# The 64-row term of the output projection as pairs of half-height matmuls in every block, and one v matmul moved a step ahead

## The chip, the core and the metric

The kernel runs on one core of one Trainium2 chip. The metric is the device time of one execution in microseconds (us): 213.64 us is the median of three runs of the kernel before (213.34 to 214.03).

## What is computed

An input x of 2048 rows and 448 columns is normalised row by row, and two branches are added to it: attention with 16 heads of 28 over a sliding window of 256 keys, and a gated feed-forward layer with 1792 hidden columns.

```python
xn = _layernorm(x)
qkv = (xn @ wqkv).reshape(B, S, 3, H, Dh).transpose(2, 0, 3, 1, 4)   # H = 16, Dh = 28
scores = einsum("bhqd,bhkd->bhqk", q, k) * Dh ** -0.5
mask = (i - j >= 0) & (i - j < 256)
o = softmax(where(mask, scores, -1e9)) @ v
return x + o @ wo + (gelu(xn @ w_gate) * (xn @ w_up)) @ w_down
```

All tensors are bf16. 448 columns are three chunks of 128 rows and one of 64 for TensorE, whose array has 128 rows; that fourth chunk is what this change is about.

## The kernel before

The 2048 rows are four blocks (`NB`) of 512 columns (`QB`), each of four output tiles of 128. For each block `attention` runs nine or ten score steps and `gated` then makes the hidden values `hT`. One score step is: scores of four heads a time into the one score buffer (`sc`, half of PSUM), the exponential on ACT into `p_sb`, and masks on DVE (`apply_masks`; on GpSimd in block 0). A `plan`, written out by hand, says what TensorE does in each step while ACT works: `(d, 12)` is twelve steps of the generator `d`. `gen_down(qb - 1)` is the output of the block before, `gen_pairs` the q, k and v of the block after, and `gen_up` part of the up projection of the present one. Steps 4 and 6 begin with the product of probabilities and v (`pv`, tile `ov`); `"sums"` and `"inverse"` are DVE's row sums and reciprocals. The other half of PSUM is four banks, `take`n and `give`n back in turn; a tile that takes a bank waits for whatever still reads it.

In `gen_down` an output tile is the sum of 14 down terms (`hT` by `wd`) and four wo terms (`oN` by `wo`), each a matmul of 448 columns; `main` and `late` name the down terms and `os` the wo terms. `end` adds x on DVE and sends the tile out. The fourth wo term has 64 real rows. For tiles 0 and 1 of blocks 0 to 2 it is computed on two halves of the array at once: tile 0 on rows 0 to 63, tile 1 on rows 64 to 127, where `o_finish` puts a copy of tile 1's columns. Tiles 2 and 3 use a full matmul, with zeros in the lower rows. In the last block all four tiles do so; its tile 3 is cut into halves of 224 columns (`first`, `last`, tile `pl`), so that little is left at the very end.

`o_collect` and `o_deliver` take the values of heads 14 and 15 through DRAM into pad rows of `oN`; `o_finish` follows them. In `mm_half` and `chunk`, too, two matmuls of 64 rows run side by side. `v_dense(t, pv)` issues the three full chunks of the v product of tile t, `v_half` its fourth; in block 0 that of tile 2 is at the head of step 1's fill.

Of the kernel before, what the change touches and what calls it, by code (L numbers as in the profile page):

```python
# [17 lines left out]
P = 128  # L18
# [9 lines left out]
def kernel(  # L28
# [185 lines left out]
    def give(*tiles):  # L214
        for ps in tiles:
            spare.append(held.pop(id(ps))[0])


    def v_dense(t, pv):
        mm3(pv, lambda c: xnT[:, c, t * P:(t + 1) * P], lambda c: wv[:, c, :], True, False)  # L220

    def v_half(t, pv):
        mm_half(pv, xnT[:, 3, t * P:(t + 1) * P], wv[:, 3, :], t % 2, False, True)
# [133 lines left out]
    def o_finish(qb):  # L357

        oN = oNs[qb]
        if qb < NB - 1:  # L360
            nc.gpsimd.memset(oN[64:128, 3, 2 * P:QB], 0.0)
            nc.gpsimd.tensor_copy(out=oN[64:128, 3, P:2 * P], in_=oN[0:64, 3, P:2 * P])
        else:
            nc.gpsimd.memset(oN[64:128, 3, :], 0.0)

    def gen_down(qb):

        hT, oN = hTs[qb], oNs[qb]
        fs = [(hT, wd, f) for f in range(NF)]
        main, late, os = fs[0:5] + fs[7:12], [fs[f] for f in (5, 12, 6, 13)], [(oN, wo, g) for g in range(4)]  # L370

        def begin(tt, lo=0, up=D):
            return tt, take("po", up - lo), lo, up

        def end(tt, po, lo, up):
            t, w = 4 * qb + tt, up - lo
            if lo:
                res = work.tile([P, 2 * QB], bf16, name="res", tag="wa", bufs=1)
            else:
                res = work.tile([P, D], bf16, name="res", bufs=4)  # L380
            nc.vector.tensor_tensor(out=res[:, 0:w], in0=po[:, 0:w], in1=x_sb[:, t, lo:up], op=ALU.add)  # L381
            if id(po) in held:
                give(po)
            nc.sync.dma_start(out=outv[:, t, lo:up], in_=res[:, 0:w])
            last_res[:] = [res]

        def part(o, terms, start=False, stop=False):
            tt, po, lo, up = o
            w = up - lo
            for n, (x, wt, k) in enumerate(terms):  # L390
                nc.tensor.matmul(po[:, 0:w], lhsT=x[:, k, tt * P:(tt + 1) * P], rhs=wt[:, k, lo:up],  # L391
                                 start=start and n == 0, stop=stop and n == len(terms) - 1, skip_group_check=True)
                if stop and n == len(terms) - 1:
                    end(*o)
                yield

        def whole(terms, *o):
            yield from part(begin(*o), terms, True, True)

        if qb < NB - 1:  # L400
            two = [begin(tt) for tt in range(2)]
            for o in two:
                yield from part(o, main + late, True)
            for o in two:
                yield from part(o, os[0:3])
            for tt, po, *_ in two:
                r = slice(64 * tt, 64 * tt + 64)
                nc.tensor.matmul(po, lhsT=oN[r, 3, tt * P:(tt + 1) * P], rhs=wo[r, 3, :], start=False, stop=True,
                                 tile_position=(64 * tt, 0), skip_group_check=True)
            for o in two:  # L410
                end(*o)
            yield
            for tt in (2, 3):
                yield from whole(main + late + os, tt)
        else:
            two = [begin(tt) for tt in range(2)]
            for terms, start in ((main, True), (late, False)):
                for o in two:
                    yield from part(o, terms, start)
            first, last = ((3, phase[0].pool.tile([P, 2, QB], f32, name="pl", tag="s")[:, 0, 0:D // 2], lo, lo + D // 2)  # L420
                           for lo in (0, D // 2))
            yield from part(first, main + late, True)
            for o in (*two, first):
                yield from part(o, os, False, True)
            yield from part(last, main, True)
            yield from whole(main + late + os, 2)
            yield from part(last, late + os, False, True)

    def new_hT(qb):
# [156 lines left out]
    def attention(qb, plan):  # L586
# [54 lines left out]
        for i, (scores, ncol, edges) in enumerate(steps):  # L641
            assert (qb, scores[-1][0]) in done
            if i in pvs:
                pv(pvs[i])
            while fresh:
                apply_masks(*fresh.pop(0))
            ss = phase[0].pool.tile([P, 4, QB], f32, name="sc", tag="s")
            p_sb = work.tile([P, 4, QB], bf16, name="p_sb", bufs=5)
            for g, half, kt, q0, nq, col in scores:
                k0, nk = (64 * half, 64) if half is not None else (0, P)  # L650
                for j in range(4):
                    r = slice(32 * j, 32 * j + Dh)
                    nc.tensor.matmul(ss[k0:k0 + nk, j, col:col + nq], lhsT=kT[r, g, kt * P + k0:kt * P + k0 + nk],  # L653
                                     rhs=qT[r, g, ring(qb).start + q0:ring(qb).start + q0 + nq], start=True, stop=True,
                                     tile_position=(32 * j, k0), skip_group_check=True)
                parts.setdefault(g, []).append((half, kt, q0, nq, col, p_sb))
            nc.scalar.activation(out=p_sb[:, :, 0:ncol], in_=ss[:, :, 0:ncol], func=ACT.Exp, scale=SCALE)  # L657
            flush()
            if qb:
                fresh.append((p_sb, edges))  # L660
            else:
                for m in edges:
                    masked(p_sb, *m)
            while later:
                scale_o(*later.pop(0))
            for n in plan[i]:
                if n == "sums":
                    sums()
                elif n == "inverse":
                    inverse()  # L670
                elif n == "masks":
                    apply_masks(*fresh.pop(0))
                elif n == "scale":
                    scale_o(*later.pop(0))
                if not isinstance(n, tuple):
                    if callable(n):
                        n()
                    continue
                for _ in range(n[1]):
                    next(n[0], None)  # L680
# [33 lines left out]
    def run(gen):  # L714
        for _ in gen:
            pass
# [13 lines left out]
    warmup(1)  # L730
    transp(1, nc.scalar.copy, "b3")
    pvs = [take("pv", D)]
    v_dense(0, pvs[0])
    norm(2)
    transp(2, nc.scalar.copy, "b2")
    norm(3)
# [5 lines left out]
    load_ffn(wu, B_w_up, slice(3, 5))  # L742
    nc.sync.dma_start(out=x_sb[:, 8:12, :], in_=xv[:, 8:12, :])
    pvs.append(take("pv", D))
    v_dense(1, pvs[1])
    pvs.append(take("pv", D, "b2"))
    pq, pk = (phase[0].pool.tile([P, 2, QB], f32, name="s0", tag="s")[:, 0, :] for _ in range(2))
    proj(pq, wqp, 0, 0)
# [13 lines left out]
    v_copy(1, pvs[1], nc.vector.tensor_copy)  # L762
    pads(nc.vector.tensor_copy, wkp, slice(1, 2))
    pvs.append(take("pv", D, "b3"))
    v_dense(3, pvs[3])
    for dst in (wqp, wkp):
        pads(nc.vector.tensor_copy, dst, slice(2, 4))

# [32 lines left out]
    for qb in range(NB):  # L801
# [4 lines left out]
        if qb == 0:  # L806
# [1 line left out]
            early = (0, 1, 2, 3, 4)  # L808
            u = chain(gen_qk((1, 2, 3), {1: (3, pvs[3]), 2: (2, pvs[2])}), gen_up(0, (1, 2, 3, 0, 4), (3, 4)))
            w = gen_pairs(1, (("v", 0), ("v", 2), ("k", 0), ("k", 1), ("k", 2)))  # L810
            plan = [[(u, 2), ahead, (u, 1)], [lambda: v_dense(2, pvs[2]), (u, 2), ahead2, (u, 1)],
                    [lambda: spare.append(spare.pop(1)), (u, 2), ahead3, (u, 4)], [lambda: stat(8), (u, 11)],
                    [lambda: stat(9), (u, 7), lambda: stat(10), (u, 7), lambda: fill_pads(True)], ["sums", (u, 7)],
                    ["inverse", "scale", (w, 11)], [(w, 10)],
# [1 line left out]
        else:  # L816
            d = gen_down(qb - 1)
            if qb < 3:
                u = gen_pairs(qb + 1, (("v", 0), ("k", 0), ("v", 2), ("k", 1), ("k", 2)))
                plan = [[(d, 14)], [(d, 11)], [(d, 11)], [(u, 7)], [(d, 18)], ["sums", (u, 7), "inverse"], [(u, 11)],  # L820
                        [lambda: q_last(qb + 1, nc.vector.tensor_copy), (d, 6), "sums"], [(d, 2), "inverse", (d, 10)],
                        [(u, 9), "masks", (u, 1)]]
                plan[3] = [(d, 1), (u, 7)]
                if qb == 2:
                    plan[0], plan[2] = [(d, 13)], [(d, 10)]
                if qb == 1:
                    for i, j in enumerate((0, 1, 2, 4)):
                        plan[j].insert(0, lambda t=12 + i: stat(t))
                    plan[4].append(lambda: rstd(12, 4))
                    plan[1] = plan[1][:1] + [lambda: q_last(1, nc.vector.tensor_copy), (d, 8)]  # L830
                    plan[2] = plan[2][:1] + [(d, 12), lambda: collect(1)]
                    plan[4].append(lambda: deliver(1))
            else:
                new_hT(3)
                early = (1, 2, 3, 4, 5, 6)
                u = gen_up(3, early, (4, 6))
                plan = [[(u, 12)], [(u, 9)], [(d, 12)], [(d, 10)], [(d, 12)], [(d, 1), (u, 7), "sums"], [(d, 12), "inverse"],
                        ["sums", "inverse", (d, 12)], [(d, 12)], [(u, 13), "masks", (u, 1)]]
        if qb in (1, 2):
            swap(qb + 1)  # L840
        score_pool(1)
# [186 lines left out]
```

## Time and profile before

| quantity | value |
|---|---|
| median of 3 runs | 213.64 us (213.34 to 214.03) |
| profiled execution | 213.22 us, span 211.5 us |
| TensorE busy | 206.6 us, 98% of the span |
| VectorE (DVE) busy | 156.8 us, 74% |
| ScalarE (ACT) busy | 131.6 us, 62% |
| GpSimd (POOL) busy | 48.9 us, 23% |
| granted TensorE clock | 1.000 |

The span runs from the first to the last instruction of the profiled execution; 1.7 us of its time lie around it. PE is TensorE's matmuls, PEld its weight loads. Matmuls are pipelined and each one's own duration overlaps with the next, so what a matmul costs is read from the distance of starts, or from the chain of work in order of time. A timeline row is: start, duration, engine, line, operation, output and inputs, shape, count, and in brackets the engine's idle time just before and what ended it.

### The profile page before, as it was taken

Reading aid. Unit: us, or ns where it says so; the run is one execution under the profiler, and the core shown is the slowest. Engines: PE = TensorE matmul, PEld = TensorE weight load, DVE = VectorE, ACT = ScalarE, POOL = GpSimd, SP = SyncE. Lnnn points to the kernel's source line nnn. Section 1 sums busy time; section 2 is a strip of 40 time slices with the busy share of each in tenths; the row PEclk is TensorE's granted clock in tenths of the full one; section 3 lists DMA queues with packets and bytes.
Section 4 is the critical chain, followed back from the end, with each engine's and each line's share of the span. In section 5 each row is a group of like instructions: output and inputs, shape, how many; then the busy total and the mean of one; then the engine's idle time right before and its main releaser. Section 6 shows DMA issues by size and latency. Waiting matters only on the chain.

```text
span 211.5 us, 6340 instructions
## 1 busy us (share of the span) xinstructions
PE 206.6 (98%) x2682; PEld 97.4 (46%) x2682; DVE 156.8 (74%) x355; ACT 131.6 (62%) x123; POOL 48.9 (23%) x86
## 2 busy tenths in 40 slices
PE   7999999999999999999999999999999999999994
PEld 2333444444454545444445444544444454544562
DVE  6899988999767985696437897395384699659722
ACT  4699488566677977413778787523577786757000
POOL 5388658451100220041000112013000022005100
PEclk9999999999999999999999999999999999999999
DMA  6999989969410101003521000100100011000011
GB/s 167 289 236 203 108 212 221 220 189 223 111 47 29 39 11 34 9 4 67 74 75 47 25 0 27 22 0 16 31 3 0 10 41 41 7 3 0 22 60 39
DMA packets 24889, 15.67 MB, mean 74 GB/s; under 512 B 9208, under 2 KB 24728, under 8 KB 24856
## 3 DMA queue, kind: packets, MB, share of 16 engines
q1 hardware_dynamic: 23814, 14.87, 32.3%
q8 instruction: 22, 0.36, 0.7%
q10 hardware_dynamic: 1042, 0.34, 0.7%
q14 instruction: 11, 0.09, 0.2%
HBM read 9.26 MB, written 2.41 MB: 55 GB/s over the span
## 4 chain that ended last, share of the span: by engine, by line
PE 94%; DVE 2%; ACT 1%; DMA 1%; issue 0%; DVEq 0%; ACTq 0%
PE po L391 24%; PE gt L457 20%; PE u L457 12%; PE ue L457 8%; PE pq L333 7%; PE sc L653 7%; PE ov L625 5%; PE pv L319 4%; PE pq L190 2%; PE pl L391 2%; DVE st L155 1%; DMA x_sb<-in_A_x_dram 1%; PE pv L190 1%; ACT p_sb L657 1%; PE s L190 1%; PE pk L190 1%
## 5 line engine op out<-in xcount | busy, mean ns | idle before, releaser
L657 ACT ACTIVATE p_sb<-sc 128x2048 bf16<-128x2048 f32 x39 | 73.2, 1878 | 20.6 <-PE sc L653 14.4
L497 ACT ACTIVATE p_sb<-gt 128x1024 bf16<-128x1024 f32 x28 | 28.7, 1024 | 33.7 <-PE gt L457 30.7
L592 POOL TENSOR_TENSOR oN<-oc,l 128x512 bf16<-128x512 f32 x16 | 21.6, 1354 | 119.0 <-DVE l L605 119.0
L457 PE MATMUL gt<-xnT,wg 64*128 64x512 bf16 x224 | 45.6, 376 | 0.0
L391 PE MATMUL po<-wd,hT 128*128 128x448 bf16 x210 | 43.3, 353 | 0.0
L457 PE MATMUL gt<-xsw,wg 64*128 64x512 bf16 x168 | 40.7, 376 | 0.0
L505 DVE TENSOR_TENSOR hT<-p_sb,u 128x512 bf16<-128x512 bf16 x34 | 21.9, 677 | 16.0 <-PE u L457 15.8
L573 DVE TENSOR_TENSOR p_sb<-p_sb,masks 128x256 bf16<-128x256 bf16 (+1 forms) x90 | 27.8, 364 | 7.6 <-ACT p_sb L657 7.6
L391 PEld LDWEIGHTS <-hT 128*128 128x128 bf16 x238 | 21.9, 98 | 19.4 <-issue 2.2
L457 PEld LDWEIGHTS <-wg 64*128 64x128 bf16 x392 | 19.0, 94 | 22.5 <-issue 0.2
L457 PEld LDWEIGHTS <-wu 64*128 64x128 bf16 x392 | 18.8, 94 | 22.4 <-issue 1.0
L457 PE MATMUL u<-xnT,wu 64*128 64x512 bf16 x136 | 28.1, 376 | 0.0
L457 PE MATMUL u<-xsw,wu 64*128 64x512 bf16 x102 | 24.7, 376 | 0.0
L457 PE MATMUL ue<-xnT,wu 64*128 64x512 bf16 x88 | 18.0, 377 | 0.0
L381 DVE TENSOR_TENSOR res<-po,x_sb 128x448 bf16<-128x448 f32 x15 | 9.0, 619 | 11.5 <-PE po L391 11.0
L653 PE MATMUL sc<-qT,kT 28*64 28x320 bf16 (+7 forms) x648 | 16.4, 261 | 0.1
L457 PE MATMUL ue<-xsw,wu 64*128 64x512 bf16 x66 | 16.3, 377 | 0.0
L583 POOL TENSOR_SCALAR_AFFINE_SELECT p_sb<-p_sb 128x512 bf16<-128x512 bf16 (+1 forms) x21 | 14.2, 705 | 5.9 <-ACT p_sb L657 5.8
L610 DVE TENSOR_TENSOR oc<-oc,ov 128x512 f32<-128x512 f32 x12 | 8.2, 681 | 8.6 <-ACT oc L609 8.6
L653 PEld LDWEIGHTS <-kT 28*64 28x64 bf16 (+1 forms) x648 | 7.5, 102 | 13.3 <-issue 12.0
L474 DVE CAST hT<-ue 128x512 bf16<-128x512 f32 x18 | 11.6, 679 | 1.8 <-PE ue L457 1.8
L391 PE MATMUL po<-wo,oN 128*128 128x448 bf16 x54 | 12.0, 352 | 0.0
(110 smaller groups left out, 278.9 us busy)
## 6 DMA issues: line engine op xcount, KB each, us to landing
out_dram<-res SPq DMA_DIRECT2D x15, 112.0 KB
wd<-in_B_w_down_dram SPq DMA_DIRECT2D x2, 784.0 KB
x_sb<-in_A_x_dram SPq DMA_DIRECT2D x3, 448.0 KB
xsw<-xnT SPq DMA_DIRECT2D x6, 192.0 KB
wu<-in_B_w_up_dram SPq DMA_DIRECT2D x4, 224.0 KB
wg<-in_B_w_gate_dram SPq DMA_DIRECT2D x2, 448.0 KB
wu<-in_B_w_up_dram SPq DMA_DIRECT2D x2, 336.0 KB
wg<-in_B_w_gate_dram SPq DMA_DIRECT2D x2, 336.0 KB
```

Source lines behind the costliest of these rows:

```text
L190: nc.tensor.matmul(ps, lhsT=lhs(c), rhs=rhs(c), start=start and c == 0, stop=stop and c == 2, skip_group_check=True)
L333: nc.tensor.matmul(ps, lhsT=w.rearrange("p h d -> p (h d)"), rhs=xchunk(qb, hi, c, qb * QB, QB), start=c == 0, stop=c == 6, tile_position= ...
L391: nc.tensor.matmul(po[:, 0:w], lhsT=x[:, k, tt * P:(tt + 1) * P], rhs=wt[:, k, lo:up], start=start and n == 0, stop=stop and n == len(term ...
L457: nc.tensor.matmul(ps, lhsT=w[64 * hi:64 * hi + 64, c, p * P:(p + 1) * P], rhs=xchunk(qb, hi, c, qb * QB, QB), start=c == 0, stop=c == 6, ...
L474: copy(out=hTs[qb][:, p + 7 * i, :], in_=us[i])
L497: nc.scalar.activation(out=ges[p][:, :, :], in_=gt[:, :, :], func=ACT.Gelu_apprx_tanh)
L505: nc.vector.tensor_tensor(out=hT[:, p + 7 * i, :], in0=ge[:, i, :], in1=u, op=ALU.mult)
L573: nc.vector.tensor_tensor(out=reg, in0=reg, in1=m, op=ALU.mult)
L583: nc.gpsimd.affine_select(out=reg, in_=reg, pattern=mid + [[1 if diag else -1, min(w, P)]], compare_op=ALU.is_ge, fill=0.0, base=0 if diag ...
L592: nc.gpsimd.tensor_tensor(out=oN[:, g, :], in0=oc[:, :], in1=inv, op=ALU.mult)
L653: nc.tensor.matmul(ss[k0:k0 + nk, j, col:col + nq], lhsT=kT[r, g, kt * P + k0:kt * P + k0 + nk], rhs=qT[r, g, ring(qb).start + q0:ring(qb) ...
L657: nc.scalar.activation(out=p_sb[:, :, 0:ncol], in_=ss[:, :, 0:ncol], func=ACT.Exp, scale=SCALE)
```

## The change

`o_finish` now copies, in every block, the columns of tiles 1 and 3 to rows 64 to 127, and fills nothing with zeros. `os` is three terms, and the fourth is issued by the new `half(hi, ...)`, on rows 0 to 63 for one tile and 64 to 127 for another.

In blocks 0 to 2 tiles 2 and 3 make such a pair. It is issued when tile 2 has all its other terms. In blocks 0 and 1 tile 3 has nothing else by then: its half term alone is added to x on DVE and parked in float32 (`xo`) in columns of `hT` that tiles 0 and 1 no longer need; later tile 3 starts afresh, and `end` adds `xo` in place of x. In block 2 tile 3 is complete, and both end there. In the last block the half terms of tiles 0, 1, 2 and of the two halves of tile 3 are issued together.

The plans follow: in blocks 1 and 2 the pair stands in step 5 behind `"sums"`, and in block 3 at the head of step 9, where step 8's masks come behind it. Statistics of row tile 15 go from step 4 to step 2 of block 1, and one copy of the up projection's pair 5 goes from DVE to ACT. In block 0 the first of the three matmuls of `v_dense(2)` goes to the head of step 0's fill.

```diff
     def v_dense(t, pv):
-        mm3(pv, lambda c: xnT[:, c, t * P:(t + 1) * P], lambda c: wv[:, c, :], True, False)
+        for c in range(3):
+            nc.tensor.matmul(pv, lhsT=xnT[:, c, t * P:(t + 1) * P], rhs=wv[:, c, :], start=c == 0, stop=False, skip_group_check=True)
+            yield
...
     def o_finish(qb):
-        if qb < NB - 1:
-            nc.gpsimd.memset(oN[64:128, 3, 2 * P:QB], 0.0)
-            nc.gpsimd.tensor_copy(out=oN[64:128, 3, P:2 * P], in_=oN[0:64, 3, P:2 * P])
-        else:
-            nc.gpsimd.memset(oN[64:128, 3, :], 0.0)
+        up, low = (oN[r, 3, :].rearrange("p (a b n) -> p a b n", b=2, n=P)[:, :, 1, :] for r in (slice(0, 64), slice(64, 128)))
+        nc.gpsimd.tensor_copy(out=low, in_=up)
...
-        main, late, os = fs[0:5] + fs[7:12], [fs[f] for f in (5, 12, 6, 13)], [(oN, wo, g) for g in range(4)]
+        main, late, os = fs[0:5] + fs[7:12], [fs[f] for f in (5, 12, 6, 13)], [(oN, wo, g) for g in range(3)]
...
+        def half(hi, o, start, stop):
+            tt, po, lo, up = o
+            r = slice(64 * hi, 64 * hi + 64)
+            nc.tensor.matmul(po[:, 0:up - lo], lhsT=oN[r, 3, tt * P:(tt + 1) * P], rhs=wo[r, 3, lo:up], start=start, stop=stop,
+                             tile_position=(64 * hi, 0), skip_group_check=True)
...
-            for tt in (2, 3):
-                yield from whole(main + late + os, tt)
+            third = begin(2)
+            yield from part(third, main + late + os, True)
+            if qb == NB - 2:
+                fourth = begin(3)
+                yield from part(fourth, main + late + os, True)
+            else:
+                fourth = begin(3)
+            half(0, third, False, True)
+            half(1, fourth, qb < NB - 2, True)
+            end(*third)
+            if qb == NB - 2:
+                end(*fourth)
+                yield
+                return
+            xo = hT[:, 0:4, 0:D // 2].bitcast(f32)
+            nc.vector.tensor_tensor(out=xo, in0=four(fourth[1]), in1=four(x_sb[:, 4 * qb + 3, :]), op=ALU.add)
+            give(fourth[1])
+            yield
+            fourth = begin(3)
+            for n, _ in enumerate(part(fourth, main + late + os, True)):
+                if n < 16:
+                    yield
+            end(*fourth, xo)
+            yield
...
+            third = begin(2)
             for o in (*two, first):
-                yield from part(o, os, False, True)
-            yield from part(last, main, True)
-            yield from whole(main + late + os, 2)
+                yield from part(o, os)
+            for hi, o in enumerate((*two, third, first, last)):
+                half(hi % 2 if hi < 4 else 1, o, o in (third, last), o not in (third, last))
+            for o in (*two, first):
+                end(*o)
+            yield from part(last, main)
+            yield from part(third, main + late + os, False, True)
             yield from part(last, late + os, False, True)
...
-            while fresh:
+            while fresh and plan[i].count("masks") < 2:
                 apply_masks(*fresh.pop(0))
...
-            plan = [[(u, 2), ahead, (u, 1)], [lambda: v_dense(2, pvs[2]), (u, 2), ahead2, (u, 1)],
+            v2 = v_dense(2, pvs[2])
+            plan = [[(v2, 1), (u, 2), ahead, (u, 1)], [(v2, 2), (u, 2), ahead2, (u, 1)],
...
-                plan = [[(d, 14)], [(d, 11)], [(d, 11)], [(u, 7)], [(d, 18)], ["sums", (u, 7), "inverse"], [(u, 11)],
-                        [lambda: q_last(qb + 1, nc.vector.tensor_copy), (d, 6), "sums"], [(d, 2), "inverse", (d, 10)],
+                plan = [[(d, 14)], [(d, 11)], [(d, 11)], [(u, 7)], [(d, 17)], ["sums", (d, 1), (u, 7), "inverse"], [(u, 11)],
+                        [lambda: q_last(qb + 1, nc.vector.tensor_copy), (d, 6), "sums"], [(d, 2), "inverse", (d, 9)],
...
-                    for i, j in enumerate((0, 1, 2, 4)):
+                    for i, j in enumerate((0, 1, 2, 2)):
                         plan[j].insert(0, lambda t=12 + i: stat(t))
...
-                u = gen_up(3, early, (4, 6))
+                u = gen_up(3, early, (4, 5, 6))
                 plan = [[(u, 12)], [(u, 9)], [(d, 12)], [(d, 10)], [(d, 12)], [(d, 1), (u, 7), "sums"], [(d, 12), "inverse"],
-                        ["sums", "inverse", (d, 12)], [(d, 12)], [(u, 13), "masks", (u, 1)]]
+                        ["sums", "inverse", (d, 11)], [(d, 11)], [(d, 1), "masks", (u, 13), "masks", (u, 1)]]
```

More of the change, by code (lines that the diff above doesn't have):

```diff
@@ L369, in gen_down, with four, end @@
         fs = [(hT, wd, f) for f in range(NF)]
-        main, late, os = fs[0:5] + fs[7:12], [fs[f] for f in (5, 12, 6, 13)], [(oN, wo, g) for g in range(4)]
+        main, late, os = fs[0:5] + fs[7:12], [fs[f] for f in (5, 12, 6, 13)], [(oN, wo, g) for g in range(3)]
         def begin(tt, lo=0, up=D):
             return tt, take("po", up - lo), lo, up
-        def end(tt, po, lo, up):
+        def four(a):
+            return a.rearrange("p (a b) -> p a b", a=4)
+        def end(tt, po, lo, up, rest=None):
             t, w = 4 * qb + tt, up - lo
@@ L380, in end @@
                 res = work.tile([P, D], bf16, name="res", bufs=4)
-            nc.vector.tensor_tensor(out=res[:, 0:w], in0=po[:, 0:w], in1=x_sb[:, t, lo:up], op=ALU.add)
+            if rest is None:
+                nc.vector.tensor_tensor(out=res[:, 0:w], in0=po[:, 0:w], in1=x_sb[:, t, lo:up], op=ALU.add)
+            else:
+                nc.vector.tensor_tensor(out=four(res[:, :]), in0=four(po), in1=rest, op=ALU.add)
             if id(po) in held:
@@ L395, in part @@
                 yield
-        def whole(terms, *o):
-            yield from part(begin(*o), terms, True, True)
+        def half(hi, o, start, stop):
[3 more added lines that the diff above has]
+                             tile_position=(64 * hi, 0), skip_group_check=True)
         if qb < NB - 1:
@@ L405, in gen_down @@
                 yield from part(o, os[0:3])
[L406 to L409, printed above, removed]
+            for hi, o in enumerate(two):
+                half(hi, o, False, True)
             for o in two:
@@ L412, in gen_down @@
             yield
-            for tt in (2, 3):
-                yield from whole(main + late + os, tt)
+            third = begin(2)
[3 more added lines that the diff above has]
+                yield from part(fourth, main + late + os, True)
+            else:
+                fourth = begin(3)
[16 more added lines that the diff above has]
+            yield
         else:
@@ L732 @@
     pvs = [take("pv", D)]
-    v_dense(0, pvs[0])
+    run(v_dense(0, pvs[0]))
     norm(2)
@@ L744 @@
     pvs.append(take("pv", D))
-    v_dense(1, pvs[1])
+    run(v_dense(1, pvs[1]))
     pvs.append(take("pv", D, "b2"))
@@ L764 @@
     pvs.append(take("pv", D, "b3"))
-    v_dense(3, pvs[3])
+    run(v_dense(3, pvs[3]))
     for dst in (wqp, wkp):
@@ L830 @@
                     plan[1] = plan[1][:1] + [lambda: q_last(1, nc.vector.tensor_copy), (d, 8)]
-                    plan[2] = plan[2][:1] + [(d, 12), lambda: collect(1)]
+                    plan[2] = plan[2][:2] + [(d, 12), lambda: collect(1)]
                     plan[4].append(lambda: deliver(1))
```

## Prediction

> **What bounds the kernel now.** I read the page first: busy shares, then the shares of the chain that ended last.
>
> ```profile
> PE 206.6 (98%) x2682; PEld 97.4 (46%) x2682; DVE 156.8 (74%) x355; ACT 131.6 (62%) x123; POOL 48.9 (23%) x86
> ...
> PE 94%; DVE 2%; ACT 1%; DMA 1%; issue 0%; DVEq 0%; ACTq 0%
> ```
>
> TensorE is busy for 98% of the 211.5 us span and makes 94% of the chain. A busy row alone would prove little, since matmuls are pipelined, but the chain in order of time shows nothing but TensorE over long stretches, so a column less streamed there should be time won, if no other engine is then late. What a column costs I read from the chain, at the end of the last block:
>
> ```profile
> 187.30 7.55 PE gt L457 x70
> 194.85 5.40 PE po L391 x28
> 200.26 1.34 PE pl L391 x14
> 201.60 1.51 PE po L391 x8
> ...
> 208.66 0.39 DVE res L381
> ```
>
> The eight wo terms of 448 columns take 1.51 us, 0.189 each; the fourteen of 224 columns take 1.34, 0.096 each. The 28 terms ahead should take 28 x 0.189 = 5.29 and show 5.40: the surplus of 0.11 stands where 64-row tiles (gt, 70 matmuls in 35 pairs, 7.55 us, 0.216 a pair) give way to full-height matmuls. I take 0.10 for such a change of tile shape.
>
> What a pair of 64-row matmuls costs is seen at the pair that exists already, in step 3 of block 1 (TensorE's timeline):
>
> ```profile
> 60.53 0.42 PE L653 MATMUL sc<-qT,kT 28*64 28x320 bf16 x16
> 60.89 0.36 PE L408 MATMUL po<-wo,oN 64*128 64x448 bf16 x2
> 61.09 0.35 PE L319 MATMUL pv<-wv,xnT 64*128 64x448 bf16 x1
> ```
>
> Both matmuls start at 60.89 and the next work at 61.09: two 448-column matmuls in 0.20 us, the price of one. The pair stands between scores and 64x128 work, so no change of shape is paid.
>
> **The change, part by part.**
>
> *Blocks 0 to 2 (executed in attention of blocks 1, 2, 3).* Tiles 2 and 3 each lose one full wo term (2 x 0.189) and get one common pair (0.19 to 0.20): 0.19 saved per block, 0.57 in three. The pairs go to the head of the fills of step 5 (blocks 1 and 2) and step 9 (block 3), behind scores and ahead of 64x128 pairs, exactly the neighbourhood of 60.89. So no shape change is added. The saving appears in the step that loses a term without getting the pair: step 8 in blocks 1 and 2, steps 7 and 8 in block 3. There the exponential could take over as the bound, because there is one score buffer:
>
> ```profile
> 69.03 0.74 PE L625 MATMUL ov<-p_sb,v_sb 64*32 64x256 bf16 x48
> ...
> 75.18 1.69 PE L391 MATMUL po<-wd,hT 128*128 128x448 bf16 x8
> 76.70 0.92 PE L391 MATMUL po<-wo,oN 128*128 128x448 bf16 x4
> 77.55 0.43 PE L653 MATMUL sc<-qT,kT 28*64 28x320 bf16 x24
> ```
>
> ```profile
> 63.77 1.88 ACT L657 ACTIVATE p_sb<-sc 128x2048 bf16<-128x2048 f32 x1
> ...
> 75.31 1.88 ACT L657 ACTIVATE p_sb<-sc 128x2048 bf16<-128x2048 f32 x1 [0.59 <-PE sc L653]
> ```
>
> Step 8's exponential ends at 75.31 + 1.88 = 77.19. The scores of step 9 start at 77.55 and would start at 77.36: still 0.17 behind the exponential, so the 0.19 is kept. Block 3 takes a term from two steps in a row:
>
> ```profile
> 175.66 1.88 ACT L657 ACTIVATE p_sb<-sc 128x2048 bf16<-128x2048 f32 x1 [0.85 <-PE sc L653]
> ```
>
> ```profile
> 177.85 0.43 PE L653 MATMUL sc<-qT,kT 28*64 28x320 bf16 x24
> ```
>
> That exponential moves forward by the first 0.19 and ends at 175.47 + 1.88 = 177.35; the scores move forward by both, to 177.47. That is 0.12 of slack, after which the pair at step 9 gives one 0.19 back. Bounds for block 3: 0.19 saved, or nothing if the exponential is later than this.
>
> *The added work on VectorE.* In blocks 1 and 2 tile 3's half sum is parked: one more add from PSUM into float32 (xo). The moves ahead of it matter more than its length. DVE of block 1, around step 5:
>
> ```profile
> 65.96 0.18 DVE L156 BATCH_NORM_AGGREGATE mv_all<-st 128x2 f32<-128x6 f32 x1
> 67.16 0.62 DVE L381 TENSOR_TENSOR res<-po,x_sb 128x448 bf16<-128x448 f32 x1 [1.02 <-PE po L391]
> 67.70 0.82 DVE L573 TENSOR_TENSOR p_sb<-p_sb,masks 128x256 bf16<-128x256 bf16 x3
> 68.44 0.70 DVE L598 STREAM_TRANSPOSE l<-oc 128x512 f32<-128x512 f32 x1
> 69.18 0.26 DVE L599 RECIPROCAL inv_all<-l 128x16 f32<-128x16 f32 x1
> ```
>
> Today the masks and sums (67.70 to 69.44, 1.74 us) are queued behind tile 2's add, which waits 1.02 us for TensorE. In the new order masks and sums come first: the exponential of step 4 ends at 63.77 + 1.88 = 65.65, and the statistics row in front is moved to step 2. So they run from about 65.7 to 67.4, inside that idle time. The step's scores start 0.19 earlier and the pair after them ends at about 67.6 (scores to end of pair, 60.53 to 61.25, is 0.72). Then tile 2's add and xo follow; for two such adds in a row there is a row:
>
> ```profile
> 61.28 1.16 DVE L381 TENSOR_TENSOR res<-po,x_sb 128x448 bf16<-128x448 f32 x2 [0.25 <-PE po L408]
> ```
>
> 1.16 from 67.6 gives 68.8. I take the same for xo, which writes the same count in float32; the bounds are 0.58 (half of this row) and 0.70 (the transposing row of 512 float32 elements). What is queued behind: the k copy of the step's pair, then the inverse; and the next product, probabilities by v at 69.03, takes the two banks that these adds free. It is 0.2 us clear, so nothing is charged. The cover gone, each 0.1 late costs 0.1 at 69.03, twice. Block 2 has more room, 1.77 us of idle:
>
> ```profile
> 117.21 0.62 DVE L381 TENSOR_TENSOR res<-po,x_sb 128x448 bf16<-128x448 f32 x1 [1.77 <-PE po L391]
> ```
>
> In block 3 the two adds stand in front of step 8's masks, which only the product of group 3, behind the gates, reads; one copy of pair 5 goes from DVE to ACT in exchange. Nothing is charged. The finishing add with xo replaces one of the same size.
>
> *The last block.* Its wo terms of chunk 3 were 3 x 0.189 + 2 x 0.096 = 0.76 us. Now they take the time of two 448-column matmuls, 0.38: tiles 0 and 1 side by side, then tile 2 beside the two 224-column halves of tile 3. That saves 0.38. But here the pairs stand between full-height matmuls, so two shape changes are added, 2 x 0.10. Net 0.18. Bounds: 0.38 if they cost nothing, 0.
>
> The Trainium skill, in TensorEngine Tiling (Array Packing), section Key Properties, says that changing the tiling mode drains TensorE; the trace agrees, with 0.11 at 194.85. Without that drain this part would give 0.38 and the whole sum 0.95.
>
> On GpSimd the fill with zeros goes and the copy doubles. In the last block the copy must now wait for the DMA that delivers the pad rows, where the fill waited only for the collect:
>
> ```profile
> 198.32 0.52 POOL L364 MEMSET oN<- 64x512 bf16 x1 [2.37 <-DMA o<-oN]
> ```
>
> ```profile
> 56.18 0.28 POOL L362 COPY oN<-oN 64x128 bf16<-64x128 bf16 x1 [2.38 <-DMA oN<-o]
> ```
>
> In block 0 that copy waited 2.38 us behind the fill. The same here: 198.32 + about 0.3 + 2.4 = 201.0, plus 0.28 to 0.56, ready by 201.6. The halves follow nine terms from 201.60 (6 x 0.189 + 3 x 0.096 = 1.42), at 203.0. Cover 1.4 us; beyond it a late copy would cost its lateness in full.
>
> *The v product of tile 2.* One of its three matmuls moves from step 1's fill to the head of step 0's, where TensorE has to wait for the first exponential. That looks like 0.19 more. But everything behind it in step 0 is then 0.19 later. DVE, ACT and TensorE, in this order:
>
> ```profile
> 13.31 0.62 DVE L226 CAST v_sb<-pv 128x448 bf16<-128x448 f32 x1
> ...
> 15.82 0.18 DVE L156 BATCH_NORM_AGGREGATE mv_all<-st 128x2 f32<-128x6 f32 x1
> ```
>
> ```profile
> 16.04 0.30 ACT L160 ACTIVATE lnv<-mv_all,eps_t 128x3 f32<-128x3 f32 x1
> ...
> 16.99 1.88 ACT L657 ACTIVATE p_sb<-sc 128x2048 bf16<-128x2048 f32 x1
> ```
>
> ```profile
> 19.11 0.40 PE L653 MATMUL sc<-qT,kT 28*128 28x128 bf16 x8
> ```
>
> DVE's v copy takes the output of step 0's fill, and DVE then runs without a gap to 16.00. ACT's logarithm follows that end by 0.04, and the exponential follows in ACT's queue. All shift by 0.19: the exponential to 17.18, its end to 19.06, and step 3's scores cannot start much before the 19.11 of today. So the 0.19 won on TensorE is waited away there. I take 0; bounds 0.19 gained (the DVE series absorbs the shift) and 0.19 lost (the shift also reaches step 3).
>
> **Sum.** 0.57 + 0.18 + 0 = 0.75 us less. The profiled execution took 213.22 us, so 212.47 for such a one; the median of the three runs is 213.64, 0.42 above it, and against that median the forecast is 212.9. The measurement can tell about 0.3%, 0.64 us. The gain is 0.35%, just over it.
>
> **The rivals.**
>
> *Slower: DVE becomes the wait in step 5.* Parking tile 3 puts two adds in front of the banks that the product at 69.03 needs. If masks and sums do not fit ahead of the pair and start only at 67.16, they end at 68.90, the adds at 70.1, and TensorE waits 1.05 us in each of two blocks: 2.1 - 0.75 = 1.35 slower, 215.0. It decides from the point where the adds start 0.6 us later than 67.6 in both blocks: 0.2 is free, and twice 0.38 is the whole gain. Against it: the idle of 1.02 and 1.77 us, and the exponential's end at 65.65. Chance 0.10.
>
> *Drains at every pair.* If each new pair paid two shape changes, 4 x 0.20 against 0.57 + 0.38 = 0.95 leaves 0.15: 213.5, no change that can be told. [...] Against it: 60.89 to 61.09 with no gap, and the places chosen. Chance 0.08.
>
> *The exponential takes back block 3 and part of the tail.* The slack of 0.12 is thin. Blocks 1 and 2 give 0.38, the tail at most 0.18 more: 213.1 to 213.3. Chance 0.12.
>
> *The v move and the tail pay in full.* 0.75 + 0.19 + 0.20 = 1.14: 212.5. For it: the tail's halves might overlap the drain. Against: the DVE series without a gap. Chance 0.15.
>
> **How the numbers follow.** The forecast has 0.55. With 0.75 against a bound of 0.64, I count 0.40 of it as faster and 0.15 as the same. Faster 0.40 + 0.15 = 0.55; same 0.15 + 0.08 + 0.12 = 0.35; slower 0.10. The range leaves out the slower case (0.10) and little else: from the full gain, 212.5, less the 0.30 by which the lowest run shown lies under the median, 212.2; up to the drain case, 213.5, plus the 0.39 of the highest run, 213.9.
>
> **What would show it.** Right: the new pairs start together, and the next 64x128 work 0.20 later, in steps 5, 5 and 9; step 9's scores in block 1 come 8.33 us behind step 6's product instead of 8.52 (69.03 to 77.55); from the first down term of the last block to the last add 13.63 us instead of 13.81 (194.85 to 208.66); step 3's scores of block 0 at 19.1 as now. Wrong: an idle row of DVE's adds as releaser ahead of the product in step 6; scores of step 9 in block 3 released by ACT; a wait for GpSimd's copy in the last block; more than 0.1 us between a pair and its successor.

## The result, and the profile after

The changed kernel took 212.75 us, median of 12 runs (212.56 to 213.13), against 213.34 us for the kernel before (12 runs, 213.18 to 214.03): ratio 0.9971, 95% interval 0.9962 to 0.9980. That is 0.59 us, 0.28%: inside the range and faster, but just under the 0.64 us that the prediction took as the line for telling a change. The profiled execution took 212.77 us, its span 211.1.

From the page of the changed kernel: span and the engines' busy time.

```profile
span 211.1 us, 6335 instructions
...
PE 205.3 (97%) x2678; PEld 96.5 (46%) x2682; DVE 157.7 (75%) x356; ACT 131.8 (62%) x124; POOL 48.3 (23%) x83
```

TensorE is busy 1.3 us less, DVE 0.9 us more. Busy time is not the gain; that is read between score groups. In the table each stretch runs from the start of one group of score matmuls (or down terms) to another in TensorE's timeline.

| stretch | before | after | difference |
|---|---|---|---|
| start of span to scores of step 0, block 0 | 11.17 | 11.47 | +0.30 |
| block 0, scores of step 0 to scores of step 3 | 7.94 | 7.89 | -0.05 |
| from there to the first scores of block 1 | 32.74 | 32.71 | -0.03 |
| first scores of block 1 to those of block 2 | 50.84 | 50.65 | -0.19 |
| first scores of block 2 to those of block 3 | 50.11 | 49.92 | -0.19 |
| first scores of block 3 to its first gate | 28.44 | 28.26 | -0.18 |
| first gate to first down term of the last block | 13.55 | 13.54 | -0.01 |
| first down term to the end of the last matmul | 13.84 | 13.68 | -0.16 |

From step 0 on 0.81 us are gone. The first line lies ahead of all changed work and hides 0.30 of it in this pair of executions.

The pair in step 5 of block 1, TensorE's timeline after:

```profile
67.09 0.42 PE L686 MATMUL sc<-qT,kT 28*64 28x320 bf16 x16
67.44 0.36 PE L405 MATMUL po<-wo,oN 64*128 64x448 bf16 x2
67.64 0.38 PE L335 MATMUL pq<-xnT,wqp 64*128 64x512 bf16 x1
...
69.25 0.74 PE L658 MATMUL ov<-p_sb,v_sb 64*32 64x256 bf16 x48
69.92 0.43 PE L686 MATMUL sc<-qT,kT 28*64 28x320 bf16 x24
```

Both matmuls of the pair start at 67.44 and the next 64x128 work 0.20 us later. DVE beside it:

```profile
65.91 0.83 DVE L606 TENSOR_TENSOR p_sb<-p_sb,masks 128x256 bf16<-128x256 bf16 x3 [0.30 <-ACT p_sb L690]
66.66 0.70 DVE L631 STREAM_TRANSPOSE l<-oc 128x512 f32<-128x512 f32 x1
67.40 0.25 DVE L632 RECIPROCAL inv_all<-l 128x16 f32<-128x16 f32 x1
67.84 0.62 DVE L384 TENSOR_TENSOR res<-po,x_sb 128x448 bf16<-128x448 f32 x1 [0.19 <-PE po L405]
68.38 0.61 DVE L434 TENSOR_TENSOR hT<-po,x_sb 128x448 f32<-128x448 f32 x1
```

Masks and sums are done 0.19 us before tile 2's add can start, which waits for the pair; the parking add (L434) takes 0.61 and ends at 68.99, before the product at 69.25, which has no idle time in its row.

Block 3, where two steps in a row lost a term: ACT's last exponential before the change, then ACT and TensorE after it.

```profile
178.44 1.88 ACT L657 ACTIVATE p_sb<-sc 128x2048 bf16<-128x2048 f32 x1 [0.90 <-PE sc L653]
```

```profile
175.32 1.88 ACT L690 ACTIVATE p_sb<-sc 128x2048 bf16<-128x2048 f32 x1 [0.66 <-PE sc L686]
177.91 1.88 ACT L690 ACTIVATE p_sb<-sc 128x2048 bf16<-128x2048 f32 x1 [0.71 <-PE sc L686]
```

```profile
177.32 0.43 PE L686 MATMUL sc<-qT,kT 28*64 28x320 bf16 x24
177.68 0.36 PE L405 MATMUL po<-wo,oN 64*128 64x448 bf16 x2
177.88 0.38 PE L490 MATMUL ue<-xnT,wu 64*128 64x512 bf16 x1
```

ACT's idle time ahead of these exponentials shrank from 0.85 and 0.90 to 0.66 and 0.71 and is still ended by TensorE; the first one ends at 177.20, 0.12 ahead of the scores.

The end of the chain in order of time, and GpSimd's copy in the last block:

```profile
194.51 5.40 PE po L396 x28
199.91 1.34 PE pl L396 x14
201.26 1.13 PE po L396 x6
202.39 0.29 PE pl L396 x3
202.68 0.39 PE po L405 x3
203.07 0.10 PE pl L405
203.17 1.06 PE pl L396 x10
204.23 3.21 PE po L396 x17
207.45 0.69 PE pl L396 x7
...
208.16 0.39 DVE res L384
```

```profile
199.70 0.39 POOL L363 COPY oN<-oN 64x256 bf16<-64x256 bf16 x1 [4.10 <-DMA oN<-o]
```

The five half terms take 0.49 (202.68 to 203.17), and the ten terms behind them 1.06 where ten of 0.096 are 0.96. That is 0.59 for the 0.38 of streaming: 0.21 for going into 64-row tiles and out again. The copy is done at 200.09, 2.5 us ahead of its first reader.

The v product: ACT and TensorE after.

```profile
16.52 0.30 ACT L160 ACTIVATE lnv<-mv_all,eps_t 128x3 f32<-128x3 f32 x1 [0.30 <-DVE mv_all L156]
...
17.43 1.88 ACT L690 ACTIVATE p_sb<-sc 128x2048 bf16<-128x2048 f32 x1
```

```profile
19.36 0.40 PE L686 MATMUL sc<-qT,kT 28*128 28x128 bf16 x8
```

Counted from step 0's scores, the exponential starts at 5.96, which was 5.82, and ends at 7.84; step 3's scores follow at 7.89, 0.05 behind it. ACT now waits for DVE's statistics in its own row.

### The profile page after: what moved, and what is told of

Read it like the earlier page. It is cut to its first block, busy times and chain, and to the rows that moved or that the text cites. A ratio compares the mean times of both kernels' runs of the same rounds, so it can differ in the third digit from the quotient of the medians.

```text
span 211.1 us, 6335 instructions
## 1 busy us (share of the span) xinstructions
PE 205.3 (97%) x2678; PEld 96.5 (46%) x2682; DVE 157.7 (75%) x356; ACT 131.8 (62%) x124; POOL 48.3 (23%) x83
## 4 chain that ended last, share of the span: by engine, by line
PE 93%; DMA 4%; DVE 1%; issue 1%; SPq 0%; DVEq 0%
PE po L396 24%; PE gt L490 20%; PE u L490 12%; PE ue L490 8%; PE sc L686 7%; PE pq L335 7%; PE ov L658 5%; PE pv L321 4%; DMA x_sb<-in_A_x_dram 4%; PE pq L190 2%; PE pl L396 2%; PE po L405 1%; PE pk L190 1%; DVE st L155 1%; PE pv L221 0%
## 5 line engine op out<-in xcount | busy, mean ns | idle before, releaser
L384 DVE TENSOR_TENSOR res<-po,x_sb 128x448 bf16<-128x448 f32 x13 | 7.7, 621 | 7.7 <-PE po L405 4.4
L507 DVE CAST hT<-ue 128x512 bf16<-128x512 f32 x17 | 11.1, 683 | 1.5 <-PE ue L490 1.4
L631 DVE STREAM_TRANSPOSE l<-oc 128x512 f32<-128x512 f32 x16 | 11.1, 693 | 0.0
```

What stands on the lines that cost most here:

```text
L507: copy(out=hTs[qb][:, p + 7 * i, :], in_=us[i])
L631: nc.vector.transpose(out=l1[:, :, :].rearrange("p a b -> p (a b)"), in_=oc[:, :])
```

## Experiments

Of each run the median is given with that of the kernel before on the same chip, and the ratio with its interval.

**The changed kernel again.** No edit.

> The changed kernel once more, unaltered. Theory: by the two traces, stretch by stretch, the change is worth 0.05 (block 0, scores of step 0 to scores of step 3: 7.94 to 7.89 us) + 3 x 0.19 + 0.16 (last block) = 0.78 us, and the profiled execution hid 0.30 of it because its first scores came at 11.47 instead of 11.17, before any changed work. If that 0.30 is chance, this trace has its first scores nearer to 11.2 and the stretches repeat to 0.03; the median is 0.6 to 0.8 below the kernel before. Rival: the later start belongs to the change; then it is 11.4 to 11.5 here too.

212.72 against 213.45 us, ratio 0.9963 (0.9949 to 0.9976). All stretches repeat to 0.01, but the first scores came at 11.50, so "nearer to 11.2" missed. The other traces tell more: the code ahead of the first scores is the same in every kernel here, and they came at 11.15 to 11.59 in the eleven with the changed blocks and at 11.17 and 11.35 in the two with the old ones. What made them late in the first trace of the changed kernel stands in its rows, DVE and TensorE:

```profile
9.27 0.63 DVE L155 BATCH_NORM_STATS2 st<-x_sb 128x6 f32<-128x448 bf16 x1 [0.50 <-DMA x_sb<-in_A_x_dram]
```

```profile
11.47 0.40 PE L686 MATMUL sc<-qT,kT 28*128 28x128 bf16 x8 [0.19 <-DVE kT L246]
```

DVE's statistics wait for a load of x, the k copy behind them is late, and the scores wait for that copy. In this second trace it is the first load of x: DVE's first statistics, which wait for it, start at 3.26 instead of 2.92 in the kernel before. The changed kernel a third time, beside the last run below:

> The changed kernel a third time, on the same chip as the run with the exchanged bank. Theory: stretches as in its other two traces (7.89; 5.46 from the scores of step 1 to those of step 3; 0.19 less than before in each of blocks 1 to 3; 13.67 at the end), the time of the first scores anywhere from 11.1 to 11.6; median 212.6 to 212.9.

212.70 against 213.39 us, ratio 0.9967 (0.9955 to 0.9979); first scores at 11.16, the stretches 7.89, 5.46, then 0.19, 0.19 and 0.18 less than before, and 13.67. So the late start comes with the loads and not with the change, as far as thirteen traces tell. In this trace 0.11 is lost again between step 3 and block 1 (32.82 instead of 32.71), within the 22 up matmuls behind step 3's scores. TensorE and DVE there:

```profile
19.82 0.80 PE L490 MATMUL ue<-xnT,wu 64*128 64x512 bf16 x4
20.38 0.47 PE L490 MATMUL ue<-xsw,wu 64*128 64x512 bf16 x2
```

```profile
19.64 0.68 DVE L246 CAST kT<-pk 128x512 bf16<-128x512 f32 x1
```

The row at 20.38 starts 0.56 behind the one ahead of it, where the first trace has 0.43, and 0.06 behind the end of DVE's k copy (20.32), which gives back a bank. Six of the thirteen traces, that of the kernel before among them, have this matmul 0.05 to 0.06 behind the copy's end; in the other seven the copy ends earlier by 0.09 or more. The wait is read from these rows; no run moved the copy. Why DVE comes to it later stays open: the six normalisations ahead of it took 2.49 us here and 1.93 in the first trace.

**The v product back.**

```diff
-            plan = [[(v2, 1), (u, 2), ahead, (u, 1)], [(v2, 2), (u, 2), ahead2, (u, 1)],
+            plan = [[(u, 2), ahead, (u, 1)], [(v2, 3), (u, 2), ahead2, (u, 1)],
```

> The changed kernel with all three matmuls of tile 2's v product back in step 1. Theory: the move gained 0.05 only, so this is 0.05 slower than the changed kernel: scores of step 0 to scores of step 3 in block 0 are 7.94 again, and the exponential of step 2 starts 5.82 behind the scores of step 0, not 5.96. Rival (the move pays in full): 0.19 slower. Rival (it costs): faster.

212.81 against 213.45 us, ratio 0.9962 (0.9947 to 0.9978). Scores of step 0 to step 3 are 7.94, the exponential of step 2 is at 5.82. The move is worth 0.05; timing alone could not have told it.

**All of it in step 0.**

```diff
-            plan = [[(v2, 1), (u, 2), ahead, (u, 1)], [(v2, 2), (u, 2), ahead2, (u, 1)],
+            plan = [[(v2, 3), (u, 2), ahead, (u, 1)], [(u, 2), ahead2, (u, 1)],
```

> The changed kernel with all three matmuls of tile 2's v product in step 0's fill. Theory: step 0 has room for about one of them (in the changed kernel TensorE ends step 0's fill just as the first exponential ends, scores of step 1 2.43 behind those of step 0 in both traces); two more push the scores of step 1 by 0.38, and DVE's series, the logarithm and the exponential of step 2 with them by 0.38: scores of step 0 to scores of step 3 in 8.2 us, 0.3 to 0.4 slower than the changed kernel. Rival (TensorE alone is the bound there): the same time, since TensorE's work is the same.

212.97 against 213.42 us, ratio 0.9985 (0.9974 to 0.9995). The scores of step 1 came 0.37 later (2.80 instead of 2.43) and those of step 3 too (8.26). TensorE's work is the same, so it is not the only bound there: what is put into step 0 above one matmul is lost in full.

**The last block alone.** The kernel before with the half terms and the copy of the last block only.

```diff
...
             for o in (*two, first):
-                yield from part(o, os, False, True)
-            yield from part(last, main, True)
-            yield from whole(main + late + os, 2)
-            yield from part(last, late + os, False, True)
+                yield from part(o, os[0:3])
+            for hi, o in enumerate((*two, third, first, last)):
+                half(hi % 2 if hi < 4 else 1, o, o in (third, last), o not in (third, last))
...
```

> The kernel before with the last block alone changed: its five half terms side by side, GpSimd's copy there in place of the zeros. Theory: from the first down term of the last block to the last add 13.65 us instead of 13.81, all other stretches as before; 0.16 us faster than the kernel before. If the change of tile shape cost nothing it would be 0.38.

213.35 against 213.45 us, ratio 0.9996 (0.9986 to 1.0005), no difference to be told by time. In the trace the last stretch is 13.67 instead of 13.84 and every other stretch that of before: 0.17.

**A pair among full-height matmuls.** Block 2's pair moves from step 9 into step 8.

```diff
                 fourth = begin(3)
-                yield from part(fourth, main + late + os, True)
+                yield from part(fourth, main + late, True)
+                half(0, third, False, True)
+                half(1, fourth, False, False)
+                end(*third)
+                yield from part(fourth, os, False, True)
+                yield
+                return
```

> The changed kernel with block 2's pair moved from the head of step 9 (behind scores, ahead of 64x128 pairs) to step 8, between full-height matmuls: behind tile 3's down terms and ahead of its three wo terms. Same work. Theory: two changes of tile shape are added, 2 x 0.10: in block 3, from the scores of step 8 to the first gate matmul 6.4 us instead of 6.2, and 0.2 us slower in all. Rival (the price at a pair's place is nothing, and the last block's missing 0.2 has another cause): no change.

212.99 against 213.42 us, ratio 0.9980 (0.9969 to 0.9991). TensorE's timeline:

```profile
174.71 0.42 PE L688 MATMUL sc<-qT,kT 28*64 28x320 bf16 x16
...
176.69 0.36 PE L405 MATMUL po<-wo,oN 64*128 64x448 bf16 x2
176.98 0.74 PE L396 MATMUL po<-wo,oN 128*128 128x448 bf16 x3
177.65 0.43 PE L688 MATMUL sc<-qT,kT 28*64 28x320 bf16 x24
...
181.05 0.38 PE L492 MATMUL gt<-xnT,wg 64*128 64x512 bf16 x1
```

Behind the pair the full-height matmuls start after 0.29, not 0.19. From the scores of step 8 to the first gate it is 6.34 us instead of 6.12. The same two matmuls cost 0.22 more because of their neighbours, 0.10 to 0.11 for each of the two changes of tile shape. The Trainium skill says in TensorEngine Tiling (Array Packing), section Key Properties, that changing the tiling mode drains TensorE; this trace agrees with it, with 0.10 us behind the pair.

**DVE made late ahead of the adds.** Statistics that nobody reads, once and twice, in step 5 of blocks 1 and 2.

```diff
-                plan = [..., ["sums", (d, 1), (u, 7), "inverse"], ...
+                plan = [..., ["sums", lambda: stat(0), (d, 1), (u, 7), "inverse"], ...     # a second lambda: stat(0) in the other kernel
```

> The changed kernel with an extra statistics of row tile 0 (0.8 us of DVE, its result not used any more) ahead of the two adds in step 5 of blocks 1 and 2. Theory: the adds, which waited 0.19 us for TensorE, start 0.6 later, so they end 0.6 later; 0.26 of that is free before the product of step 6 needs their banks, so that product comes 0.3 to 0.4 later in each of the two blocks: 0.6 to 0.8 slower than the changed kernel. Rival (the product does not hang on these adds): no change.

> The same with two such extra statistics, 1.6 us. Theory: each further us of DVE comes through in full: another 0.8 per block, 1.1 to 1.2 per block, 2.2 to 2.4 slower than the changed kernel. Rival (no hanging on these adds): no change.

Once: 213.20 against 213.42 us, ratio 0.9989 (0.9980 to 0.9999). Twice: 214.62 against 213.42 us, ratio 1.0050 (1.0035 to 1.0066), slower than the kernel before. Block 1 with two, DVE and TensorE:

```profile
69.09 0.59 DVE L384 TENSOR_TENSOR res<-po,x_sb 128x448 bf16<-128x448 f32 x1
69.60 0.61 DVE L434 TENSOR_TENSOR hT<-po,x_sb 128x448 f32<-128x448 f32 x1
```

```profile
69.73 0.29 PE L658 MATMUL ov<-p_sb,v_sb 64*32 64x256 bf16 x4 [0.32 <-DVE res L384]
70.26 0.73 PE L658 MATMUL ov<-p_sb,v_sb 64*32 64x256 bf16 x44 [0.24 <-DVE hT L434]
```

The product waits for both adds by name: this is the rival that would have made the change slower. With one extra statistics the adds started 0.42 and 0.49 later behind their pair and step 6's scores 0.18 and 0.25; with two, 1.15 and 1.21 later, and the scores 0.91 and 0.98. The difference is 0.24, 0.24, 0.24 and 0.23: so much was free, and every us beyond it is lost. Both expectations were too high (0.3 to 0.4, and 1.1 to 1.2 per block): one statistics delays what follows it on DVE by 0.70, not 0.8, and its row starts 0.08 before the reciprocal's ends, so the adds came 0.42 and 0.49 later, not 0.6.

**The statistics out of the way.**

```diff
     def ahead2():
-        stat(6)
         stat(7)
...
-            plan = [[(v2, 1), (u, 2), ahead, (u, 1)], ...
+            plan = [[(v2, 1), (u, 2), ahead, lambda: stat(6), (u, 1)], ...
```

> The changed kernel with the statistics of row tile 6 one step earlier (step 0 of block 0, where DVE waits 0.38 us for TensorE). Theory: the v move's gain is waited away because DVE's statistics hold up ACT's logarithm, and that the exponential of step 2. With 0.8 us of DVE work taken out of that series the logarithm follows the exponential of step 1, the exponential of step 2 starts 0.15 to 0.25 earlier, and TensorE is the bound again: scores of step 0 to scores of step 3 in 7.70 us instead of 7.89, about 0.19 faster than the changed kernel. Rival: DVE's k copy, 0.4 later in step 0, then holds the scores of step 2: no gain or a loss of 0.1.

212.65 against 213.45 us, ratio 0.9963 (0.9950 to 0.9977), but 7.90 in the trace: no gain over the changed kernel. DVE, TensorE and ACT:

```profile
14.00 0.59 DVE L228 CAST v_sb<-pv 128x448 bf16<-128x448 f32 x1
```

```profile
14.10 0.55 PE L221 MATMUL pv<-wv,xnT 128*128 128x448 bf16 x2
14.65 0.81 PE L190 MATMUL pq<-xnT,wqp 128*128 128x512 bf16 x3
```

```profile
17.13 1.88 ACT L690 ACTIVATE p_sb<-sc 128x2048 bf16<-128x2048 f32 x1
```

The exponential did move, from 5.96 to 5.79 behind step 0's scores. But the q product starts 0.55 behind two v matmuls of 0.19 each, when DVE's v copy (14.00 to 14.59) has freed a bank. The rival was right that DVE's lateness in step 0 takes the gain, and wrong in the place: not the k copy but the v copy's bank. So that bank was given to the k product:

```diff
-            plan = [..., [(v2, 2), (u, 2), ahead2, (u, 1)],
+            plan = [..., [lambda: spare.insert(1, spare.pop(0)), (v2, 2), (u, 2), ahead2, (u, 1)],
```

> The run with the earlier statistics, and besides the order of two free banks exchanged at the head of step 1 of block 0: the q product of group 2 takes the bank that ACT's q copy freed, and the k product the one that DVE's v copy frees. In the run with the earlier statistics the exponential of step 2 did start 0.17 earlier against the scores of step 0 (5.79 instead of 5.96), but TensorE's q product of step 1 waited for the bank of DVE's v copy, which the statistics had pushed back. Theory: with the other bank TensorE does not wait; scores of step 2 at 5.05 to 5.07 behind the scores of step 0, and scores of step 3 at 7.72 to 7.78 (the larger of the exponential's end, 5.79 + 1.88 + 0.05, and TensorE's own fill, 5.05 + 2.70), against 7.89 in the changed kernel: 0.1 to 0.17 faster than it by the trace, which the median can hardly tell. Rival (something else holds step 1 or step 3): 7.89 again.

212.77 against 213.41 us, ratio 0.9970 (0.9957 to 0.9984). Its trace says nothing about the whole stretch (8.17), since DVE had to wait for a weight load in step 0:

```profile
12.40 0.28 DVE L745 COPY wkp<-wraw 128x336 bf16<-128x336 bf16 x1 [0.60 <-DMA wraw<-in_A_wqkv_dram]
```

> The kernel of the run before once more, because its trace fell on an execution in which DVE waited 0.60 us for a weight load in step 0 (the k pad copy at 12.40), so that scores of step 0 to scores of step 3 (8.17) says nothing there. From the scores of step 1 on it did give the 0.14 (5.32 us to the scores of step 3 instead of 5.46). Theory: without that wait the whole stretch is 7.75, and from the scores of step 1 5.32 again. Rival: the 5.32 came only because the late start left the statistics more time; then 5.4 to 5.5.

212.57 us against 212.70 of the changed kernel beside it; ratio to before 0.9961 (0.9948 to 0.9975). TensorE and ACT:

```profile
13.97 0.55 PE L221 MATMUL pv<-wv,xnT 128*128 128x448 bf16 x2
14.36 0.81 PE L190 MATMUL pq<-xnT,wqp 128*128 128x512 bf16 x3
```

```profile
16.85 1.88 ACT L690 ACTIVATE p_sb<-sc 128x2048 bf16<-128x2048 f32 x1
```

The q product follows after 0.39 instead of 0.55, the scores of step 2 come at 5.05, the exponential at 5.64, and the scores of step 3 at 7.75 behind step 0's (5.32 behind step 1's): 0.14 less than the changed kernel, 0.19 less than the kernel before, which is what the v move looked to be worth at first sight. The chain of DVE, ACT and a bank is shown to be what had held it back. The same two edits without the v move were not run; that they would gain nothing there is argued from TensorE's own work: with the product back, step 2's scores stand at 5.24 and 2.70 us of matmuls follow, which makes the 7.94. By time this version and the changed kernel can't be told apart.

## Why the prediction was right, step by step

**The pairs of blocks 0 to 2**, 0.57 forecast: 0.19 + 0.19 + 0.18 measured, in the steps named. The pair's own price next to 64x128 work stayed 0.19 to 0.20, and the exponentials stayed 0.12 ahead in block 3, the very slack worked out. The sign named for block 1 came out too: step 9's scores 8.33 behind step 6's product (69.25 to 77.58). The rival in which ACT takes this back is refuted by its idle rows. The moves that came with the pairs (the statistics of tile 15, the copy of pair 5) were not run without them, so the 0.56 belongs to all of them together.

**DVE's cover in step 5.** Forecast: masks and sums inside the old idle time, adds from 67.6 to 68.8, 0.2 of cover. Measured: 67.84 to 68.99 in a trace 0.22 later as a whole, and 0.24 of cover by the runs that made DVE late. The slower rival was the right mechanism at the right place; it decides, worked out, from about 0.6 us per block (0.24 free and 0.81 / 2), as the prediction had it; one extra statistics (0.42 and 0.49) left the kernel on the faster side and two (1.15 and 1.21) pushed it over.

**The last block**, 0.18: measured 0.16 to 0.17, also alone (from the first down term to the last add 13.65 us, with 13.63 forecast). The two changes of tile shape cost 0.21; both the rival that saw them at every pair (its price is right, its places are not) and the one that had them free are refuted. GpSimd's copy came 1.3 us earlier than estimated (199.70, not 201.0), though the trace as a whole was only 0.35 ahead by then: taking over block 0's whole wait of 2.38 behind the fill was too much.

**The v product**, 0 forecast, 0.05 measured, with the waits in the order given: DVE's statistics, ACT's logarithm, the exponential, the scores of step 3. The rival in which it pays in full needed two more edits.

**The sum.** 0.75 forecast, 0.81 and 0.82 by the first two traces of the changed kernel from step 0 on and 0.71 by the third, in which TensorE waits for the k copy; the medians gave 0.59, 0.73 and 0.69 in three comparisons. That the forecast of 212.9 lies so near the measured 212.75 is partly luck: it was taken from the median of three runs, 213.64, and the median of twelve is 0.30 lower, while the first comparison gave 0.16 less gain than the sum, and the two nearly cancel. The step that was weak is the last: 0.35% was called just over what can be told, with 0.40 of the forecast's 0.55 put on the faster side, and the gain lies on that line, under it in the first comparison and over it in the two others. The prediction did not reckon with the first loads, which move the start by up to 0.4 us from one execution to the next, half of the gain.

## What to carry to other kernels

In this kernel, on an engine that is busy throughout, a gain of a few columns could be forecast to some hundredths of a us by placing each new instruction by its neighbours: two matmuls on half the array cost one, and 0.21 to 0.22 us more when they stand between full-height ones. Before an instruction is moved into another engine's wait, follow what comes behind it on the other engines to the next common wait; here 0.14 of 0.19 came back only after a statistics and a bank had been moved as well. Where a stretch of the trace repeats to 0.01 us and the whole time scatters by 0.5, compare stretches, and look first whether a load or a copy was late in one of them.

## What the runs showed of the hardware that was not expected

The time from the start of the span to the first scores was 11.15 to 11.59 us in thirteen profiled executions, with the same code up to there; an early start can meet the next load (0.60 us of waiting at 12.40, and 0.23 in the run with the pair among full-height matmuls, whose stretch from step 0 to step 3 was 8.02 instead of 7.89). The free time ahead of a product that waits for two banks came out the same, 0.23 to 0.24, from four different delays of 0.42 to 1.21 us.
